# Three late attention units loaded in short runs and scored in 64 rows, a new order of the last output, and new lists for the first block

## The chip, the cores and the metric

The kernel runs on one core of a Trainium2 chip. The metric is device time in microseconds (us) of one execution; the kernel before takes 1649.12 us in the median of three runs (1648.95 to 1649.36).

Engines are named as the profile names them: PE is TensorE (matmul), PEld its weight loads, DVE is VectorE, ACT is ScalarE, POOL is GpSimd, SP is SyncE, which here only issues transfers. "SPq" and "ACTq" are the queues of transfers (DMAs) issued by SP and by ACT.

## The reference, cut to what matters

Three stages follow each other on 4608 tokens of width 512:

```python
# 1. attention in chunks of 64: q, k, v are (8 batches, 8 heads, 576, 64)
scores = scale * np.matmul(q_c, k_c.transpose(0, 1, 2, 4, 3))
attn = softmax(scores)                      # max subtracted, sum + 1e-9
out = np.matmul(attn, v_c)                  # -> x, (4608, 512)
# 2. gated layer, w_gate and w_val (512, 1536), w_out (1536, 512)
xn = x / sqrt(mean(x * x) + 1e-6) * rms_g
x = (silu(xn @ w_gate) * (xn @ w_val)) @ w_out
# 3. second layer, w_in (512, 2048), w_out (2048, 512)
h = x @ w_in
out = (h * clip(h + 3, 0, 6) / 6) @ w_out
```

## The kernel before

**Blocks.** The tokens go in nine blocks of 512. Every large matmul is done in split precision: an operand is a high and a low part of a narrower type, and three matmuls (high times high, low times high, high times low) make one product. From the third block on two blocks are multiplied together in a scheme that needs seven products where eight would be plain; the work of such a pair p is a row of `product` steps (the L1016 matmuls) and then 24 output steps (the triples L1030, L1031, L1033).

**The first block** runs from two lists written out by hand: `START` (attention of the first four 128-token tiles, mixed with the preparation of the first weights) and `FIRST` (the gated layer of block 0, mixed with more preparation). A token is one step: `scores1` is the scores of tile 1, `warm1` a matmul with no use for the result that keeps PE active, `Wm4`, `Wb4`, `Wh4`, `Wl4` the four steps that turn raw weight 4 into its high and low part (`Wb` is L201, L203 and L205 on DVE, `Wl` is L222 on DVE), `T` one tick of the general schedule (next paragraph). `LOADS` is the order of the first transfers. Each engine takes its instructions in the order of the list.

**The later attention** is cut into units of 256 tokens, numbered 4 to 17, and runs inside the ticks of the large products. Steps stand at fixed distances from a unit's first tick (`STEPS_P`): `turn_q` at 0, `turn_k` at 1 (a 32x32 transposition on DVE of the q and k that were loaded), scores at 3 and 5, values at 13. A unit is one of two classes:

- `Wide` loads q and k in runs of 2 KB with 8 DMAs (L886) of 128 KB each if the unit lies in one batch, with 16 smaller ones if a batch border cuts it. Its contraction over 64 is done in two accumulating matmuls of 32 rows, so the scores come in two groups of 64 matmuls (L910), at distance 3 and at distance 5, with a maximum (L921) after each.
- `Pair` loads q and k in runs of 128 bytes with 32 DMAs (L750) of 32 KB, and with 64 of 16 KB if a batch border cuts the unit in the middle, as it cuts 4 and 13. Its scores are one group of 32 matmuls of 64 rows (L781; the profile counts 64 records), all at distance 3, with one maximum (L791).

Units 4 to 9 are `Pair`; of the later ones those in `WHOLE`.

**Transfers.** q and k have one buffer each. The loads of unit i + 1 are handed to a supply when `turn_k` of unit i is issued, and each tick takes three DMAs from the supply (`some(3)`); whatever is left when `turn_q` of the unit comes is issued at once (`until`). The weights (`wo`, L463; `wd`, L469; 512 KB each) go on the same SP queue between them. SP takes its DMAs strictly in program order. The built program gives every DMA of SP and ACT one of eight completion semaphores in turn, and a DMA waits for the one that had its semaphore before, that is for the landing of the DMA eight places ahead of it.

**The end.** The last block's output accumulates in two halves of the features, m = 0 and m = 1. `last_out(m, cols, mid)` is 24 matmuls (L1796), and advances `mid` after the 15th. `tail` and `half_tail` scale a result into `c` on ACT (L1623, L1809), transpose it on PE (L1626, L1813), copy it and store it.

Of the kernel before, what the change touches and what calls it, by code (L numbers as in the profile page):

```python
# [18 lines left out]
def _f32_of(word):  # L19
# [7 lines left out]


LOADS = """
    q1 q3 q0 q2 w v3 w g w w v1 v0 v2 w w w w w w w w w w w w  # L30
""".split()
START = """
    warm2 warm2 warm2 warm2 warm2 warm2 warm2 warm2 warm2 warm2 trans_qk1 warm2 warm2 trans_qk3 out_k1 out_q1
    out_q3 out_k3 scores1 scores3 trans_qk0 warm2 trans_qk2 top1 top3 less3 less1 out_q0 expo3 out_k0 expo1 out_k2
    out_q2 total3 total1 share3 share1 scores0 warm1 warm1 warm1 warm1 scores2 trans_p3 top0 less0 top2 less2 Wm0
    out_p3 expo0 warm1 warm1 warm1 warm1 trans_p1 values3 out_p1 expo2 Wm1 out_x3 square3 total0 Wb0 total2 Wb1
    share0 share2 warm0 warm0 warm0 warm0 warm0 warm0 warm0 warm0 warm0 warm0 warm0 warm0 warm0 warm0 warm0 warm0
    warm0 warm0 warm0 warm0 mean3 trans_p0 warm2 warm2 warm2 warm2 warm2 warm2 warm2 warm2 values1 trans_p2 Wm2
    table3 out_p0 root3 Wm3 Wh0 out_p2 Wb2 inv3 values0 warm3 warm3 values2 spread3 out_x1 square1 square2 out_x2
    square0 mean1 mean2 root1 out_x0 root2 Wb3 norm3 inv1 inv2 warm3 warm3 warm3 spread1 mean0 spread2 root0 norm1  # L40
    inv0 warm3 warm3 warm3 warm3 warm3 spread0 norm2 norm0 Wm4 Wm6 hi3 hi1 hi2 hi0 Wh1 Wm5 Wh3 Wh2 lo3 Wl0 lo2 Wb6
    Wl1 Wl2 Wb4 Wl3 Wb5 lo1 lo0 warm1 warm1 warm1 warm1 warm1 warm1 warm1 warm1 warm1 warm1 warm1 warm1 warm1
    warm1 warm1 warm1 warm1 warm1 warm1 warm1
""".split()
FIRST = """
    G0 V0 T T S0 T M0 G1 T T Wm9 Wm8 Wm7 Wh4 T Wh5 A0 Wh6 Wb8 Wl4 Wb9 L0 Wl5 Wm10 Wm11 Wm13 S1 Wh9 V1 T M1 Wb10
    Wl6 Wb7 Wl9 A1 Wh7 Wh8 Wh10 L1 Wl7 D0 G2 Wb11 Wl8 V2 S2 D1 Wh11 Wm12 T M2 Wb13 Wm15 A2 Wl10 Wb12 G3 Wm19 Wm14
    Wh13 V3 Wl11 T L2 T Wh12 S3 Wl13 Wb14 Wl12 Wb15 Wb19 M3 D2 Wm18 T Wm16 Wh14 Wh15 G4 Wb18 A3 T Wm17 Wl14 L3
    Wb16 Wm22 S4 Wh18 Wm21 Wm25 V4 Wh16 T Wl15 Wb17 M4 Wb22 T Wl16 D3 T G5 Wh17 Wh22 A4 Wm24 L4 Wb25 Wb21 Wl17 V5
    T Wh19 S5 D4 Wm20 Wm26 Wh21 T Wm23 G6 Wl19 M5 Wb24 A5 Wl18 T Wb20 L5 Wl22 Wm31 Wh20 Wl20 V6 S6 T Wb26 Wl21 M6  # L50
    Wb23 A6 Wh23 Wh26 Wm27 Wh24 D5 T Wb31 L6 Wl26 Wb27 Wl23 T G7 V7 T S7 Wm28 D6 Wm33 T Wm29 Wm30 Wh25 G8 Wl24 M7
    Wb28 Wl25 A7 L7 Wb29 Wh27 T S8 V8 Wl27 M8 Wm32 Wh29 Wh28 A8 T Wb30 Wl29 Wl28 Wb33 T L8 Wm35 Wh33 Wm34 D7 G9
    Wb34 T V9 Wh30 T S9 D8 Wl33 Wl30 M9 Wh31 T T Wb32 G10 V10 T A9 Wh34 L9 Wl34 Wl31 Wh32 S10 M10 Wb35 Wl32 T A10
    D9 G11 T L10 S11 T V11 M11 D10 Wh35 A11 Wl35 L11 X T D11 T
""".split()
SHARE_V, LOW_V = (), (2, 3)

WHOLE = (10, 14)

STEPS_P = (  # L60
    (0, ("turn_q",)),
# [30 lines left out]
def fused_kernel(  # L92
# [20 lines left out]
    N = 512  # L113
# [983 lines left out]
    with tc.manual_schedule():  # L1097
# [8 lines left out]
        first = [Att(i) for i in range(NTL)]  # L1106
# [15 lines left out]

        unit = [(Pair if i < 10 or i in WHOLE else Wide)(i) for i in range(NPR)]
        chain = [Half(i) for i in range(NTL, 2 * NTL)] + unit[4:]
# [37 lines left out]
        def plan_unit(i, t0):  # L1162
            for d, steps in STEPS_H if i < NTL else STEPS if t0 < P0 else STEPS_P:
                for st in steps:
                    if i in WHOLE and st in ("scores0", "top0"):
                        st = st[:-1]
                    elif i in WHOLE and st in ("scores1", "top1"):
                        continue
# [44 lines left out]
        S00, S01, S11, S3, S1, S2, S4 = range(7)  # L1213
# [77 lines left out]
        A11, S2_, S1_, S3_, A12, S4_, A21, A22 = range(8)  # L1291
# [80 lines left out]
        for p in range(3):  # L1372
            b = 3 + 2 * p
            bk = {0: (2, 3), 1: (6, 7), 4: (4, 5)} if p % 2 == 0 else {0: (6, 7), 1: (2, 3), 4: (4, 5)}
            g = {}
# [11 lines left out]
            def bank(z, m):  # L1387
                return PS[:, bk[z][m], :]
# [3 lines left out]
            for i in range(NI + 1):  # L1392
# [5 lines left out]
                end = [(2, 0), (7, 0), (2, 1), (7, 1)]  # L1398
# [88 lines left out]
        X = {}  # L1487
# [133 lines left out]
        def tail(m, blk, h):  # L1621
            c, *o = [wp.tile([128, 2, N], F32, tag="w", name=n)[:, 0, :] for n in ("c", "ot", "ot")]
            nc.scalar.mul(c, bank(Z1, m), 1.0 / 6.0)  # L1623
            yield
            for n in range(NTL):
                nc.tensor.transpose(  # L1626
                    PS[:, ZT[n // 2], n % 2 * 128:(n % 2 + 1) * 128],
                    c[:, n * 128:(n + 1) * 128],
                    ident,
                )  # L1630
            f = h * 256 + m * 128
            for y, (e, q) in enumerate(((nc.scalar.copy, nc.scalar), (nc.vector.tensor_copy, nc.sync))):
                two = o[y][:, 0:256].rearrange("p (n f) -> p n f", n=2)
                e(two, PS[:, ZT[y], 0:256].rearrange("p (n f) -> p n f", n=2))
                r = blk * N + y * 256
                q.dma_start(out=out[r:r + 256, f:f + 128].rearrange("(n p) f -> p n f", p=128), in_=two)
# [30 lines left out]
        for b in range(1, NB, 2):  # L1667
# [5 lines left out]
            end = [(2, 0), (7, 0), (2, 1), (7, 1)]  # L1673
# [119 lines left out]
        def last_out(m, cols, mid):  # L1793
            for i in range(NQ):
                for wi, xi in ((0, 0), (1, 0), (0, 1)):
                    nc.tensor.matmul(  # L1796
                        bank(Z1, m)[:, cols],
                        stream.t[pb, "out", i // 2, O22][:, i % 2, wi, m * 128:(m + 1) * 128],
                        nx[i][xi][:, cols],
                        start=False,  # L1800
                        stop=False,
                        skip_group_check=True,
                    )
                if i == NQ // 2:
                    next(mid, None)

        def half_tail(y):
            c, o = [wp.tile([128, 2, N], F32, tag="w", name=n)[:, 0, 0:256] for n in ("c", "ot")]
            nc.scalar.mul(c, bank(Z1, 1)[:, y * 256:(y + 1) * 256], 1.0 / 6.0)  # L1809
            yield  # L1810
            z = PS[:, ZT[y], 256:512]
            for n in range(2):
                nc.tensor.transpose(z[:, n * 128:(n + 1) * 128], c[:, n * 128:(n + 1) * 128], ident)  # L1813
            e, q = ((nc.scalar.copy, nc.scalar), (nc.vector.tensor_copy, nc.sync))[y]
            two = o.rearrange("p (n f) -> p n f", n=2)
            e(two, z.rearrange("p (n f) -> p n f", n=2))
            r = b * N + y * 256
            q.dma_start(out=out[r:r + 256, 384:512].rearrange("(n p) f -> p n f", p=128), in_=two)

        last_out(0, slice(0, N), iter(()))  # L1820
        end = tail(0, b, 1)
        next(end)
        for y in range(2):
            last_out(1, slice(y * 256, (y + 1) * 256), end)
            end = half_tail(y)
            next(end)
        next(end, None)


# [28 lines left out]
```

## Time and profile before

| | us |
|---|---|
| median of three runs | 1649.12 |
| the profiled execution | 1649.82 |
| its span, first to last instruction | 1648.0 |
| PE busy in the span | 1636.9 |
| DVE, ACT, POOL busy | 1034.8, 846.0, 453.4 |
| granted TensorE clock, mean | 1.00 |

The 1.82 us between the profiled time and the span lie outside the instructions. Everything below is in us from the span's start. Roughly, `START` lasts to 33.5, `FIRST` to 155, the single blocks to 366, the first pair's products and outputs to 565, the other pairs to 915, and the second layer to the end.

### The profile page before, as it was taken

The numbers are of one execution on the slowest core, as the hardware profiler recorded it, in microseconds if no ns is written. First come the engines' busy times: TensorE is split into PE (matmuls) and PEld (weight loads), VectorE is DVE, ScalarE is ACT, GpSimd is POOL, SyncE is SP. The second block draws the span as 40 slices with busy tenths as digits, with TensorE's granted clock in tenths as the row PEclk, the third lists the DMA queues.
The fourth block names the chain that finished last, engine by engine and source line by source line (L and its number), as shares of the span: only waits on it lengthen the run. The fifth ranks groups of instructions, "written<-read, shape, count | busy, mean of one in ns | idle before, by whom it ended". The sixth has DMA issues, their size and how long they took to land.

```text
span 1648.0 us, 26265 instructions
## 1 busy us (share of the span) xinstructions
PE 1636.9 (99%) x9807; PEld 1348.0 (82%) x9807; DVE 1034.8 (63%) x1532; ACT 846.0 (51%) x1410; POOL 453.4 (28%) x331
## 2 busy tenths in 40 slices
PE   8999999999999999999999999999999999999998
PEld 7888887888888888788888888888888888888887
DVE  7997566655575755638334388358746764874475
ACT  6885445455454555645434344455545544654553
POOL 1002434322236423354226522140024003301310
PEclk9999999999999999999999999999999999999999
DMA  9914777748988698855979685667877796788666
GB/s 294 287 46 108 206 211 208 209 157 243 313 277 231 203 295 269 282 216 209 331 238 334 258 283 198 219 194 244 216 216 228 213 239 200 219 230 230 191 202 156
DMA packets 352223, 375.06 MB, mean 228 GB/s; under 512 B 201440, under 2 KB 277216, under 8 KB 351968
## 3 DMA queue, kind: packets, MB, share of 16 engines
q1 hardware_dynamic: 282208, 302.32, 60.2%
q10 hardware_dynamic: 69888, 71.06, 12.7%
q8 instruction: 78, 1.28, 0.3%
q14 instruction: 49, 0.40, 0.1%
HBM read 292.55 MB, written 80.74 MB: 227 GB/s over the span
## 4 chain that ended last, share of the span: by engine, by line
PE 93%; DVE 2%; DMA 2%; SPq 2%; issue 1%; ACT 1%; POOL 0%; ACTq 0%; DVEq 0%; POOLq 0%
PE PS L1016 37%; PE PS L1595 18%; PE PS L1005 13%; PE PS L1030 6%; PE PS L1031 6%; PE PS L1033 6%; SPq L750 1%; PE PS L1042 1%; PE PS L1039 1%; PE PS L1038 1%; PE PS L837 1%; DMA q<-in_q_dram 1%; PE PS L1796 1%; PE PS L819 1%; PE PS L910 1%
## 5 line engine op out<-in xcount | busy, mean ns | idle before, releaser
L1016 PE MATMUL PS<-xu,wo 128*128 128x512 f32 x1512 | 349.8, 391 | 0.7 <-DVE s L1370 0.7
L1016 PEld LDWEIGHTS PS<-xu,wo 128*128 128x128 f32 x1512 | 282.3, 188 | 60.3 <-DVE s L1370 1.1
L1016 PE MATMUL PS<-xo,wq 128*128 128x512 f32 x1344 | 305.3, 389 | 0.0
L1595 PE MATMUL PS<-gs,wq 128*128 128x512 f32 x1296 | 295.3, 389 | 0.0
L1016 PEld LDWEIGHTS PS<-xo,wq 128*128 128x128 f32 x1344 | 252.3, 188 | 52.4
L1595 PEld LDWEIGHTS PS<-gs,wq 128*128 128x128 f32 x1296 | 242.9, 188 | 51.8 <-DVE gs L1589 1.2
L1005 PE MATMUL PS<-XH,w 128*128 128x512 f32 x576 | 146.2, 395 | 1.0 <-DVE w L222 1.0
L1005 PEld LDWEIGHTS PS<-XH,w 128*128 128x128 f32 x576 | 106.2, 188 | 24.6 <-DVE w L222 1.8
L1030 PE MATMUL PS<-gs,wd 128*128 128x512 f32 x288 | 113.2, 393 | 0.0
L1031 PE MATMUL PS<-gs,wd 128*128 128x512 f32 x288 | 112.2, 390 | 0.0
L1061 POOL TENSOR_TENSOR al<-sg,ah 128x512 fp32r<-128x512 f32 x40 | 55.9, 1396 | 155.7 <-ACT ah L1059 149.9
L1366 POOL TENSOR_TENSOR gs<-gu,gs 128x512 fp32r<-128x512 f32 x60 | 84.5, 1427 | 46.2 <-ACT gs L1365 36.3
L1370 DVE TENSOR_TENSOR gu<-gu,PS 128x512 f32<-128x512 f32 x60 | 41.1, 686 | 84.4 <-ACT gu L1452 44.1
L1663 POOL TENSOR_TENSOR gt<-gx 128x512 f32<-128x512 f32 x8 | 10.4, 1294 | 296.5 <-DVE gx L1660 296.5
L1589 DVE TENSOR_TENSOR gs<-gu,gs 128x512 fp32r<-128x512 f32 x88 | 68.0, 792 | 31.9 <-ACT gs L1588 31.6
L1588 ACT CAST gs<-gt 128x512 fp32r<-128x512 f32 x96 | 58.2, 623 | 44.1 <-DVE gt L1732 30.7
L1525 DVE SCALAR_TENSOR_TENSOR gu<-gu,PS 128x512 f32<-128x512 f32 x48 | 32.8, 684 | 72.9 <-ACT gu L1522 72.9
L1005 PE MATMUL PS<-XL,w 128*128 128x512 f32 x288 | 77.2, 390 | 0.0
L1033 PE MATMUL PS<-gs,wd 128*128 128x512 f32 x288 | 77.0, 389 | 0.0
L1059 ACT CAST ah<-sg 128x512 fp32r<-128x512 f32 x52 | 32.4, 624 | 75.5 <-DVE sg L1350 41.3
L1588 ACT CAST gs<-gu 128x512 fp32r<-128x512 f32 x96 | 57.3, 620 | 25.0 <-DVE gs L1589 17.7
L1663 POOL TENSOR_TENSOR gt<-gu 128x512 f32<-128x512 f32 x24 | 32.6, 1359 | 129.0 <-DVE gu L1660 124.8
(254 smaller groups left out, 2828.0 us busy)
## 6 DMA issues: line engine op xcount, KB each, us to landing
wq<-stash_in SPq DMA_DIRECT2D x128, 512.0 KB
wo<-ops SPq DMA_DIRECT2D x126, 512.0 KB
wq<-sums_out SPq DMA_DIRECT2D x64, 512.0 KB
wq<-stash_out SPq DMA_DIRECT2D x48, 512.0 KB
wd<-keep_out SPq DMA_DIRECT2D x36, 512.0 KB
yd<-yst SPq DMA_DIRECT2D x18, 512.0 KB
ops<-w ACTq DMA_DIRECT2D x36, 256.0 KB
v<-in_v_dram SPq DMA_DIRECT2D x32, 256.0 KB
```

What stands on the lines that cost most here:

```text
L1005: nc.tensor.matmul(ps, w(wi, c), xs[c][xi], start=(i == 0), stop=(i == n - 1))
L1016: nc.tensor.matmul(PS[:, bank, :], op[:, wi, c * 128:(c + 1) * 128], x[xi][:, c, :], start=first and i == 0, stop=last and i == 5, skip_gr ...
L1030: nc.tensor.matmul(ps, wm[0], a[0], start=first, stop=False)
L1031: nc.tensor.matmul(ps, wm[1], a[0], start=False, stop=False)
L1033: nc.tensor.matmul(PS[:, banks[m], :], w[:, 0, m * 128:(m + 1) * 128], a[1], start=False, stop=last)
L1061: nc.gpsimd.tensor_tensor(lo, t, hi.bitcast(F32), op=ALU.subtract)
L1366: e.tensor_tensor(w[:, 1, :], t, w[:, 0, :].bitcast(F32), op=ALU.subtract)
L1370: nc.vector.tensor_tensor(o, x, y, op=op)
L1588: nc.scalar.copy(w[:, 0, :], x)
L1589: e.tensor_tensor(w[:, 1, :], x, w[:, 0, :].bitcast(F32), op=ALU.subtract)
L1595: nc.tensor.matmul(PS[:, banks[m], :], op[:, wi, m * 128:(m + 1) * 128], x[xi], start=first and (wi, xi) == (0, 0), stop=False, skip_group ...
L1663: nc.gpsimd.tensor_tensor(slot(i, "t"), slot(i, "12"), slot(i, "11"), op=ALU.subtract)
```

## The change

1. `WHOLE` grows from (10, 14) to (10, 12, 13, 14, 17): units 12, 13 and 17 become `Pair`.
2. The last output is done as half of m = 1, the whole of m = 0, the other half of m = 1; before it was the whole of m = 0 and then the two halves.
3. `LOADS`, `START` and `FIRST` are new orders of the same steps, with 77 warm matmuls where there were 79, and with six `Wb` tokens in `START` where there were seven. The rest of the program is the same.

```diff
 LOADS = """
-    q1 q3 q0 q2 w v3 w g w w v1 v0 v2 w w w w w w w w w w w w
+    q1 q3 q2 q0 w w g v3 w v1 w v0 v2 w w w w w w w w w w w w
 START = """
...
-    out_q3 out_k3 scores1 scores3 trans_qk0 warm2 trans_qk2 top1 top3 less3 less1 out_q0 expo3 out_k0 expo1 out_k2
+    out_q3 out_k3 scores1 scores3 trans_qk2 warm1 trans_qk0 top1 less1 top3 less3 expo1 out_q2 out_k2 expo3 out_q0
...
-    inv0 warm3 warm3 warm3 warm3 warm3 spread0 norm2 norm0 Wm4 Wm6 hi3 hi1 hi2 hi0 Wh1 Wm5 Wh3 Wh2 lo3 Wl0 lo2 Wb6
-    Wl1 Wl2 Wb4 Wl3 Wb5 lo1 lo0 warm1 warm1 warm1 warm1 warm1 warm1 warm1 warm1 warm1 warm1 warm1 warm1 warm1
+    warm3 warm3 warm3 warm3 warm3 warm3 spread2 norm0 norm2 Wh3 Wh0 hi1 Wh2 hi3 hi0 hi2 Wm5 Wm4 Wm8 Wl0 lo3 lo2
+    Wl1 Wl2 Wb5 Wl3 Wb8 lo1 lo0 warm1 warm1 warm1 warm1 warm1 warm1 warm1 warm1 warm1 warm1 warm1 warm1 warm1
...
 FIRST = """
-    G0 V0 T T S0 T M0 G1 T T Wm9 Wm8 Wm7 Wh4 T Wh5 A0 Wh6 Wb8 Wl4 Wb9 L0 Wl5 Wm10 Wm11 Wm13 S1 Wh9 V1 T M1 Wb10
+    G0 V0 T T S0 T M0 Wb4 G1 Wm9 Wh8 A0 Wh4 Wm7 Wm6 Wb9 Wl4 L0 Wb6 V1 T Wm13 Wh5 S1 T T Wm10 Wh6 Wl5 M1 Wb7 Wl6 D0
...
-WHOLE = (10, 14)
+WHOLE = (10, 12, 13, 14, 17)
...
-        last_out(0, slice(0, N), iter(()))
+        last_out(1, slice(0, 256), iter(()))
+        first = half_tail(0)
+        next(first)
+        last_out(0, slice(0, N), first)
         end = tail(0, b, 1)
         next(end)
-        for y in range(2):
-            last_out(1, slice(y * 256, (y + 1) * 256), end)
-            end = half_tail(y)
-            next(end)
+        last_out(1, slice(256, N), end)
+        end = half_tail(1)
+        next(end)
         next(end, None)
```

**Where instructions move: SP in the first pair.** These are SP's DMAs around the loads of unit 13 before the change; L886 loads q and k, `wo` and `wd` are weights.

```order
L886 DMA q<-in_q_dram 16x2x512 x3
L463 DMA wo<-ops_123 128x1024
L463 DMA wo<-ops_124 128x1024
L886 DMA q<-in_q_dram 16x2x512 x5
L886 DMA k<-in_k_dram 16x2x512
L463 DMA wo<-ops_124 128x1024 x2
L886 DMA k<-in_k_dram 16x2x512 x3
L463 DMA wo<-ops_124 128x1024
L886 DMA k<-in_k_dram 16x2x512 x4
L463 DMA wo<-ops_124 128x1024 x2
L469 DMA wd<-keep_out_125 128x1024
```

In the changed program the loads of unit 13 begin at the same place; after 24 of its q loads and the same seven `wo` SP goes on as follows, up to the v of the next unit.

```order
L469 DMA wd<-keep_out_125 128x1024
L469 DMA wd<-keep_out_126 128x1024
L750 DMA q<-in_q_dram 32x4x32 x6
L469 DMA wd<-keep_out_127 128x1024
L469 DMA wd<-keep_out_128 128x1024
L750 DMA q<-in_q_dram 32x4x32 x2
L750 DMA k<-in_k_dram 32x4x32 x4
L469 DMA wd<-keep_out_129 128x1024
L469 DMA wd<-keep_out_130 128x1024
L750 DMA k<-in_k_dram 32x4x32 x3
L469 DMA wd<-keep_out_131 128x1024
L750 DMA k<-in_k_dram 32x4x32 x25
```

The 16 loads were all ahead of the first `wd`; now 64 loads share the queue with seven `wo` and seven `wd`, and the last 25 of them stand in a row, put there by the `until` of unit 13's `turn_q`.

**PE at the end.** The last matmuls before the change:

```order
L1796 MATMUL PS<-gs,wq 128x512 x24
L1796 MATMUL PS<-gs,wq 128x256 x15
L1626 MATMUL PS<-ident,c 128x128 x4
L1796 MATMUL PS<-gs,wq 128x256 x24
L1813 MATMUL PS<-ident,c 128x128 x2
L1796 MATMUL PS<-gs,wq 128x256 x9
L1813 MATMUL PS<-ident,c 128x128 x2
```

and after it:

```order
L1796 MATMUL PS<-gs,wq 128x256 x24
L1796 MATMUL PS<-gs,wq 128x512 x15
L1813 MATMUL PS<-ident,c 128x128 x2
L1796 MATMUL PS<-gs,wq 128x512 x9
L1796 MATMUL PS<-gs,wq 128x256 x15
L1626 MATMUL PS<-ident,c 128x128 x4
L1796 MATMUL PS<-gs,wq 128x256 x9
L1813 MATMUL PS<-ident,c 128x128 x2
```

The matmuls are the same; the 512-wide ones now lie between the two 256-wide groups, and each scaled copy `c` is made while the next group runs.

**DVE at the start.** The first instructions of DVE, as a difference (`mx` is the maximum of a tile's scores, `v` the scores less it):

```order
 L1090 MEMSET one 128x1
 L1091 CAST ones_r<-one 128x256
-L546 TENSOR_REDUCE mx<-PS 128x8 x2
-L552 TENSOR_TENSOR v<-PS,mx 128x512 x2
+L546 TENSOR_REDUCE mx<-PS 128x8
+L552 TENSOR_TENSOR v<-PS,mx 128x512
+L546 TENSOR_REDUCE mx<-PS 128x8
+L552 TENSOR_TENSOR v<-PS,mx 128x512
 L560 TENSOR_REDUCE sm<-v 128x8
```

The two maxima no longer follow each other, and the first one now waits for a later place of PE's stream: in the changed list `warm1`, which writes the bank of tile 1, stands behind the eight transposes of `trans_qk2` and ahead of `top1`.

## Rows read from the trace of the kernel before

**Rows 1.** The page: PE's busy time, and its costliest wait.

```profile
PE 1636.9 (99%) x9807; PEld 1348.0 (82%) x9807; DVE 1034.8 (63%) x1532; ACT 846.0 (51%) x1410; POOL 453.4 (28%) x331
L1005 PE MATMUL PS<-XH,w 128*128 128x512 f32 x576 | 146.2, 395 | 1.0 <-DVE w L222 1.0
```

**Rows 2.** Timeline of PE around groups of scores: start, duration, instruction, count.

```profile
377.29 1.16 PE L781 MATMUL PS<-kT,qT 64*64 64x64 f32 x64
462.68 1.16 PE L910 MATMUL PS<-kT,qT 32*64 32x64 f32 x64
463.77 5.75 PE L1016 MATMUL PS<-xu,wo 128*128 128x512 f32 x24
469.45 1.16 PE L910 MATMUL PS<-kT,qT 32*64 32x64 f32 x64
505.63 1.16 PE L910 MATMUL PS<-kT,qT 32*64 32x64 f32 x64
```

**Rows 3.** Chain that ended last, a stretch of products that nothing interrupts.

```profile
366.46 10.89 PE PS L1016 x48
```

**Rows 4.** Timeline of PE and of DVE at the end: [idle before, releaser].

```profile
1631.11 7.39 PE L1796 MATMUL PS<-gs,wq 128*128 128x512 f32 x39
1631.42 1.89 DVE L1589 TENSOR_TENSOR gs<-gt,gs 128x512 fp32r<-128x512 f32 x3
...
1640.48 2.05 PE L1796 MATMUL PS<-gs,wq 128*128 128x256 f32 x15 [0.47 <-ACT c L1809]
```

**Rows 5.** Timelines of DVE and PE in the first 40 us.

```profile
1.25 2.50 PE L640 MATMUL PS<-ones_r 128*128 128x256 f32 x10 [1.25 <-DVE ones_r L1091]
...
8.27 1.43 DVE L546 TENSOR_REDUCE mx<-PS 128x8 f32<-128x512 f32 x2 [7.08 <-PE PS L535]
...
9.65 0.36 PE L640 MATMUL PS<-ones_r 128*128 128x256 f32 x1
...
16.16 2.66 PE L640 MATMUL PS<-ones_r 128*128 128x256 f32 x20
...
35.45 1.20 PE L1005 MATMUL PS<-XH,w 128*128 128x512 f32 x4 [0.77 <-DVE w L222]
...
35.92 0.42 DVE L201 TENSOR_SCALAR wtmp<-wtmp 128x512 f32<-128x512 f32 x1
36.37 0.43 DVE L203 TENSOR_SCALAR wtmp<-wtmp 128x512 uint32<-128x512 uint32 x1
36.83 0.69 DVE L205 SCALAR_TENSOR_TENSOR wraw<-wraw,wtmp 128x512 uint32<-128x512 uint32 x1
```

**Rows 6.** Windows inside `FIRST`: length, busy time (instructions) by engine, clock, DMA share, GB/s.

```profile
60.00:80.00 20.00, 20.00 (x152) 16.17 (x151) 19.13 (x39) 15.62 (x39) 0.00 (x0) 1.00 0.94 307
```

**Rows 7.** Timeline of SP: issue of the first, until the last, DMA, count.

```profile
123.06 16.32 SPq L750 DMA_DIRECT2D k<-in_k_dram  x32
...
415.71 1.28 SPq L886 DMA_DIRECT2D q<-in_q_dram  x3
...
460.51 1.28 SPq L886 DMA_DIRECT2D q<-in_q_dram  x3
...
479.00 0.84 SPq L463 DMA_DIRECT2D wo<-ops  x2
...
501.94 1.42 SPq L750 DMA_DIRECT2D q<-in_q_dram  x3
...
514.59 9.35 SPq L750 DMA_DIRECT2D k<-in_k_dram  x14
```

**Rows 8.** Waits of SP's queue from 455 to 530: us in total, times, longest.

```profile
SPq L469 <- DMA wo<-ops: 3.8, 2, 2.0
```

**Rows 9.** Chain from 150 to 180, a transfer of 256 KB from issue to landing.

```profile
174.38 2.22 DMA ops<-oh
```

**Rows 10.** Transpositions on DVE: timeline before unit 13's loads, and group of the short form.

```profile
458.22 2.27 DVE L890 STREAM_TRANSPOSE qT<-q 128x1024 f32<-128x1024 f32 x1
L762 DVE STREAM_TRANSPOSE kT<-k 128x1024 f32<-128x1024 f32 x8 | 9.7, 1209 | 0.0
```

More of the change, by code (lines that the diff above doesn't have):

```diff
@@ L29 @@
 LOADS = """
-    q1 q3 q0 q2 w v3 w g w w v1 v0 v2 w w w w w w w w w w w w
+    q1 q3 q2 q0 w w g v3 w v1 w v0 v2 w w w w w w w w w w w w
 """.split()
 START = """
-    warm2 warm2 warm2 warm2 warm2 warm2 warm2 warm2 warm2 warm2 trans_qk1 warm2 warm2 trans_qk3 out_k1 out_q1
-    out_q3 out_k3 scores1 scores3 trans_qk0 warm2 trans_qk2 top1 top3 less3 less1 out_q0 expo3 out_k0 expo1 out_k2
-    out_q2 total3 total1 share3 share1 scores0 warm1 warm1 warm1 warm1 scores2 trans_p3 top0 less0 top2 less2 Wm0
@@ L36 @@
[L36 to L40, printed above, removed]
@@ L41 @@
-    inv0 warm3 warm3 warm3 warm3 warm3 spread0 norm2 norm0 Wm4 Wm6 hi3 hi1 hi2 hi0 Wh1 Wm5 Wh3 Wh2 lo3 Wl0 lo2 Wb6
-    Wl1 Wl2 Wb4 Wl3 Wb5 lo1 lo0 warm1 warm1 warm1 warm1 warm1 warm1 warm1 warm1 warm1 warm1 warm1 warm1 warm1
+    warm0 warm0 warm0 warm0 warm0 warm0 warm0 warm0 warm0 warm0 trans_qk1 warm0 warm0 trans_qk3 out_k1 out_q1
+    out_q3 out_k3 scores1 scores3 trans_qk2 warm1 trans_qk0 top1 less1 top3 less3 expo1 out_q2 out_k2 expo3 out_q0
+    out_k0 total1 total3 share1 share3 scores2 warm3 warm3 scores0 trans_p1 warm3 warm3 warm3 warm3 trans_p3 top2
@@ new lines @@
+    less2 top0 less0 out_p1 expo2 Wm0 out_p3 expo0 warm2 warm2 warm2 warm2 warm2 warm2 warm2 warm2 warm2 warm2
+    warm2 values3 warm0 warm0 warm0 warm0 warm0 warm0 warm0 warm0 warm0 warm0 warm0 warm0 warm0 warm0 warm0 warm0
+    values1 Wm1 out_x3 table3 square3 Wm2 square1 out_x1 total2 Wb0 total0 Wb1 share2 share0 trans_p2 mean3
+    trans_p0 mean1 root3 out_p2 out_p0 root1 Wm3 Wb2 inv3 inv1 warm2 values0 spread3 values2 square0 out_x0
+    square2 out_x2 warm1 mean0 spread1 mean2 root0 Wh1 root2 Wb3 norm3 inv0 norm1 inv2 spread0 warm3 warm3 warm3
@@ L45 @@
 FIRST = """
-    G0 V0 T T S0 T M0 G1 T T Wm9 Wm8 Wm7 Wh4 T Wh5 A0 Wh6 Wb8 Wl4 Wb9 L0 Wl5 Wm10 Wm11 Wm13 S1 Wh9 V1 T M1 Wb10
[L47 to L54, printed above, removed]
+    G0 V0 T T S0 T M0 Wb4 G1 Wm9 Wh8 A0 Wh4 Wm7 Wm6 Wb9 Wl4 L0 Wb6 V1 T Wm13 Wh5 S1 T T Wm10 Wh6 Wl5 M1 Wb7 Wl6 D0
+    A1 Wh7 Wh9 Wm14 T Wm11 Wl7 L1 Wl8 Wb10 G2 Wb13 V2 D1 T T S2 Wb14 Wl9 M2 Wm15 T Wh10 Wm18 Wm12 A2 G3 Wb15 Wl10
+    L2 Wb11 Wb12 T Wh13 Wm16 Wh11 V3 D2 S3 Wm19 Wb18 Wl11 Wb16 Wl13 M3 Wh18 Wh14 T Wh12 Wl12 Wh16 Wh15 Wm21 A3
+    Wl15 Wl18 L3 G4 Wm22 S4 T Wm17 V4 Wl14 Wl16 Wb19 Wb21 M4 Wb17 A4 Wm20 Wh17 Wh21 D3 T T Wl17 L4 Wb22 Wb20 G5 V5
+    Wm26 T S5 Wm23 D4 Wb23 M5 Wh19 T A5 Wm29 Wh20 Wh22 G6 Wb26 Wb29 T Wm27 Wl22 Wl19 L5 Wh29 Wh23 S6 V6 T Wl20
+    Wl21 M6 Wb27 Wm28 Wm24 Wh26 Wm32 A6 T Wl23 Wb24 L6 Wl26 D5 G7 T V7 Wm25 T D6 Wh24 S7 Wh27 T G8 Wl24 Wb25 M7
+    Wl29 Wh25 Wb28 Wl25 Wb32 Wm33 Wm31 A7 T Wb31 L7 Wm30 S8 V8 T Wb33 Wb30 M8 Wl27 A8 Wh28 Wm35 Wh30 D7 L8 T Wl28
+    T G9 V9 T S9 Wh31 Wm34 D8 T G10 Wb35 M9 Wb34 A9 Wl30 T L9 T Wl31 Wh33 V10 S10 Wh32 M10 Wl33 Wl32 Wh34 A10 Wh35
+    T D9 G11 Wl34 L10 Wl35 S11 V11 T D10 T M11 T A11 L11 X D11 T
 """.split()
 SHARE_V, LOW_V = (), (2, 3)
-WHOLE = (10, 14)
+WHOLE = (10, 12, 13, 14, 17)
 STEPS_P = (
```

## The prediction

> **What bounds the kernel now.** I read the page first: PE is busy 1636.9 of 1648.0 us, and of its few waits the largest kind after the start is 1.0 us in all, for prepared weights [rows 1]. So only three things can move the time: matmuls that PE no longer does, waits at the two ends of the program where PE isn't yet or no longer covered, and a new wait that is put into the covered middle. Then I read the timeline of PE around the groups of scores [rows 2, 3], the two ends [rows 4, 5], and last the queue of SP, because the three changed units load q and k in four times as many DMAs as before, 32, 64 and 32 instead of 8, 16 and 8 [rows 7, 8]. The reader is to see there that SP's is the only queue whose work this change multiplies.
>
> **Scores: −4.0 us.** A `Wide` unit's second group starts 1.09 us before the products go on (462.68 to 463.77 [rows 2]). It also interrupts them: the 24 products between the two groups take 5.68 us (463.77 to 469.45 [rows 2]) where 24 uninterrupted ones take 10.89 / 2 = 5.45 [rows 3], so another 0.23. A `Pair` unit's single group of 64 records takes 1.16 us like one of the two [rows 2]. So a unit saves 1.09 + 0.23 = 1.32 us, three of them 4.0, all on PE, which never waits there. DVE's part (transposition 1.21 instead of 2.2 us [rows 10]) gets shorter too, and hides.
>
> **Last output: −0.5 us.** Before, PE stood 0.47 us between the two halves until ACT had scaled the first [rows 4]. Now 15 matmuls of 512 columns lie over that copy, and the copy of m = 0 lies under 15 of 256 columns, which took 2.05 us [rows 4]. The last half with its copy, transposes and store is as before. What could eat this: the half pass goes through its operands twice as fast, and the last of them come out of DVE at 1633.31 (1631.42 + 1.89 [rows 4]). The last output starts at 1631.11, and at the pace of 15 matmuls in 2.05 us [rows 4] the half pass is at its 17th of 24 by then, about where it needs them. I keep bounds of −0.7 and +0.3.
>
> **Start lists: +1.0 us.** DVE sets the pace up to the first real matmul. Before, its first maximum starts at 8.27; in the changed list it waits for a warm matmul behind eight transposes, and that place of PE's stream was over at 9.65 + 0.36 = 10.01 [rows 5]. That is 1.7 later. One `Wb` less in `START` takes 0.42 + 0.43 + 0.69, less the overlaps 1.4 us, off DVE [rows 5]; so the first matmuls come 0.3 later. That step is now done in `FIRST`, where DVE is busy 19.13 of 20 us [rows 6]: of its 1.4 us half may come through to PE, 0.7. The wait of 0.77 for prepared weights [rows 5] is for the same kind of step as before, and I leave it in. Bounds: −1.0 if both waits of [rows 1] go and `FIRST` hides all, +2.5 if it hides nothing.
>
> **Loads of units 12 and 17: 0.** Each has 32 DMAs of 32 KB instead of 8. Unit 12's begin at 415.71 [rows 7] with some 12 weight loads between; at the 0.65 us derived below, 44 DMAs are through by 444.3, and `turn_q` stood at 458.22 [rows 10]. Unit 17 has the same distance one pair later. If they had no such room, each microsecond late would be one of PE.
>
> **Loads of unit 13: +7.9 us.** The q buffer comes free when unit 12 has been transposed: 458.22 + 1.2 [rows 10], so the first of the 64 is issued at about 459.5. PE wants the scores at 505.63 [rows 2], 1.32 sooner by unit 12's saving: 504.3 (the shift of the start moves both). Between stand 64 loads and 14 weight loads, 78 DMAs, in program order. What does one cost? Nothing else to carry: 32 in 16.32 us, 0.51 each, of the same size [rows 7]. Beside weights, in the next unit: from 501.94 to 523.94 (514.59 + 9.35) SP issued 16 q, 14 k and four `wd`, 34 in 22.0 us, 0.65; its k alone 14 in 9.35, 0.67 [rows 7]. In the very stretch, 460.51 to 479.84, it issued 16 q and k of 64 KB and seven `wo`, 23 in 19.3 us, 0.84 [rows 7]. The surplus over 0.51 is the wait for the DMA eight places ahead: SP waited there for the landing of `wo`, up to 2.0 us at a time [rows 8]. So I take 0.65 for the 53 DMAs up to the last `wd` of this stretch, 34.4 us, to 493.9; and 0.59, midway between 0.51 and 0.67, for the 25 k in a row, which only ACT's transfers disturb, 14.8 us, to 508.7. Landing takes 2.2 us more (a 256 KB transfer did, [rows 9]; I have no row for a small one), `turn_k` 1.2 [rows 10] and 0.1 of handing over: the scores can start at 512.2, and PE stands 7.9 us. It takes its instructions in order, and behind the scores it has only the outputs of this pair, so nothing fills the hole. By the cheapest row (0.51 throughout) the scores are ready at 499.3 + 3.5 = 502.8 and the wait is nothing; by the dearest (0.84 for the 53, then 0.67) at 524.3, and it is 20.
>
> **Sum.** −4.0 − 0.5 + 1.0 + 7.9 = +4.4. On the profiled execution (1649.82, 0.70 above the median shown) 1654.2; on the median 1649.12 it is 1653.5, +0.27%. A measurement of this kernel tells about 0.2%, 3.3 us, from no change.
>
> **Rivals.**
> - *SP keeps its unloaded pace, and nothing stalls.* It decides at (504.3 − 3.5 − 459.5) / 78 = 0.53 us per DMA: at or under that, PE never waits, and the time is 1649.12 − 3.5 = 1645.6, faster. For it: unit 4's loads, of this very shape, went at 0.51 [rows 7]. Against it: they had no weight loads between them, and every stretch with weights shows 0.65 or more. Chance 0.28, and it falls on both sides of the bound of 0.2% (1645.8) by what the start lists do.
> - *A small stall,* 1 to 5 us, from a pace of 0.54 to 0.59: 1646.6 to 1650.6, no change that can be told. Chance 0.17.
> - *The pause also costs clock.* In the first microseconds, after PE had been idle, ten warm matmuls took 2.50 us, 0.21 apart from the first on, where later 20 took 2.66, 0.12 apart [rows 5]; these are the two levels, 1.2 and 2.4 GHz (the granted-clock column says 1.00 in every slice and doesn't show it). The slow ones reach past 3.3 us, and the single one at 9.65 is too late to tell. If the stall puts PE back to 1.2 GHz for as long as that start shows at least (1.25 to 3.75), half of that stretch, 1.3 us, is lost, and about 2.5 if it lasts twice as long: 1654.8 to 1656. No pause in the trace after the start is longer than 1 us, so no row tells whether it happens. The Trainium skill, page "TensorE: Matmul & The Clock Gate", section "HAM oscillation — how this bites in real kernels", says that a PE which waits for DMA between stretches of matmuls falls back to the lower clock and starts the next stretch at it; by that rule the sum would be these 1.3 to 2.5 us higher. Chance 0.25, together with a stall of the size forecast.
> - *A long stall,* 11 to 20 us, by the dearest row, with weights for the next steps late behind it: 1657 to 1666. Chance 0.08.
> - *The forecast itself,* a stall of 5 to 11 us and no more: 1650.6 to 1656.6, chance 0.22 alone and 0.47 with the one that also loses clock, which shares its place and its mechanism.
>
> **How the numbers follow.** The likeliest is the stall of about 8 us: 1653.5. The range has to reach to the case without a stall, 1645.6 less half a microsecond for the lists, 1645, and up to a stall of 12 with lost clock, 1661; that leaves some 2 in 10 out. The likeliest case's own range is 1650 to 1658. Faster by over 0.2%: the part of the first rival with hidden lists, 0.22. Within 0.2%: the rest of it, the small stalls and the low end of the forecast, 0.28. Slower: 0.50.
>
> **What would show it.** In the profile after: half as many L910 groups as before, six instead of twelve, three more of L781, and products without a break where the second groups were; no wait of PE for `c` between the halves; SP's row of 25 k of unit 13 ending near 508, a `turn_k` (L762) just behind the last landing, and a wait of PE at L781 near 504 with kT of L762 as releaser, followed by matmuls at twice their spacing if the clock fell. The first L1005 near 34 and the end of `FIRST` about 1 us later. I am wrong if SP issues those 78 DMAs at 0.53 us each or faster, if PE waits at units 12 or 17 instead, or if the lists move the first block by more than 2.5 us.

## The result, and the profile after

The changed kernel takes 1662.41 us in the median of five runs (1660.34 to 1666.58), the kernel before beside it 1649.36 (1648.95 to 1652.23): a ratio of 1.0078, 95% interval 1.0066 to 1.0090. It is 13 us slower, where 4.4 us slower were forecast. The profiled execution took 1663.08 us, its span 1661.3.

The page's first line and PE's costliest waits of the changed kernel (in a list of waits: us in all, times, longest):

```profile
PE 1637.8 (99%) x9613; PEld 1349.1 (81%) x9613; DVE 1025.1 (62%) x1529; ACT 847.0 (51%) x1410; POOL 455.4 (27%) x331
```

```profile
PE PS L781 <- DVE kT L762: 11.8, 1, 11.8
PE PS L519 <- DMA q<-in_k_dram: 2.5, 2, 2.2
PE PS L1005 <- POOL XL L647: 1.6, 1, 1.6
PE PS L640 <- DVE ones_r L1091: 1.2, 1, 1.2
PE PS L1016 <- DMA wo<-ops: 1.0, 1, 1.0
```

PE has 194 instructions fewer than in [rows 1] (three second groups of 64 and two warm matmuls), and one new wait of 11.8 us, longer than all of its waits in the trace of before together. It is the one at unit 13's scores. Timelines of SP, DVE and PE there:

```profile
463.46 1.33 SPq L750 DMA_DIRECT2D q<-in_q_dram  x3
...
496.36 1.77 SPq L469 DMA_DIRECT2D wd<-keep_out  x2
498.50 1.36 SPq L750 DMA_DIRECT2D k<-in_k_dram  x3
499.95 0.65 SPq L469 DMA_DIRECT2D wd<-keep_out  x1
500.65 14.76 SPq L750 DMA_DIRECT2D k<-in_k_dram  x25
```

```profile
502.95 1.23 DVE L762 STREAM_TRANSPOSE qT<-q 128x1024 f32<-128x1024 f32 x1
519.03 1.25 DVE L762 STREAM_TRANSPOSE kT<-k 128x1024 f32<-128x1024 f32 x1 [14.86 <-DMA v<-in_v_dram]
```

```profile
507.50 1.07 PE L1033 MATMUL PS<-gs,wd 128*128 128x512 f32 x4
520.33 1.99 PE L781 MATMUL PS<-kT,qT 64*64 64x64 f32 x64 [11.76 <-DVE kT L762]
522.25 0.79 PE L1030 MATMUL PS<-gs,wd 128*128 128x512 f32 x1
522.84 0.63 PE L1031 MATMUL PS<-gs,wd 128*128 128x512 f32 x1
523.26 0.63 PE L1030 MATMUL PS<-gs,wd 128*128 128x512 f32 x1
...
525.18 1.07 PE L1033 MATMUL PS<-gs,wd 128*128 128x512 f32 x4
```

One chain explains it: q is there in time (its transposition at 502.95), the issue of the last of the 25 k in a row ends at 515.41, k is transposed 3.6 us later, and PE goes on at 520.33. (The profile infers what ended a wait from semaphores, and loads of k and v use the same ones; the transposition reads k and not v.) Then the scores take 1.99 us instead of 1.16 [rows 2], and the next matmuls start 0.43 apart, where the same ones were 0.23 apart before (507.06, 507.29, 507.52 in that trace): PE is on the lower clock. The windows of that stretch say so too (length, busy time and instructions of PE, PEld, DVE, ACT, POOL, granted clock, DMA share, GB/s):

```profile
500.00:510.00 10.00, 8.57 (x38) 6.76 (x36) 3.25 (x3) 1.92 (x3) 3.04 (x3) 1.00 0.60 177
510.00:515.00 5.00, 0.00 (x0) 0.00 (x0) 0.00 (x0) 0.00 (x0) 0.00 (x0) 0.58 0.22 34
515.00:520.00 5.00, 0.00 (x0) 0.00 (x0) 0.97 (x1) 1.69 (x3) 2.49 (x2) 0.50 0.92 243
520.00:525.00 5.00, 4.67 (x72) 4.04 (x73) 3.63 (x6) 1.38 (x3) 1.26 (x1) 0.56 1.01 298
525.00:530.00 5.00, 5.00 (x24) 4.14 (x23) 0.34 (x1) 0.94 (x2) 3.80 (x3) 1.00 0.96 265
```

From 510 to 520 not one matmul runs, the granted clock falls to the lower level (0.50), and the DMA engines are at 0.22 of their time in the first half: what PE waits for is small transfers being issued one by one, not bandwidth. The chain that ended last shows SP at it in the burst, and the list of SP's waits from the first load of unit 13 to the last what else it did:

```profile
511.19 0.43 SPq L750
511.66 0.43 SPq L750
```

```profile
SPq L750 <- DMA wd<-keep_out: 5.3, 4, 2.7
SPq L750 <- DMA wo<-ops: 3.4, 4, 1.1
```

From 504.97 on SP starts a load every 0.47 us without a wait, 0.43 of it issuing. Over the whole stretch (463.46 to 515.41, 52.0 us) its waits for landings add up to 14.3 us and those for PE to 1.0, which leaves 0.47 for each of the 78 transfers.

I set the same PE instructions of the two traces beside each other and read how much later each starts: 2.4 us at the first L1005, 3.9 at the first product (366), 2.9 behind unit 12's scores, 14.7 at unit 13's scores and 16.5 from the sixth matmul behind them on, 15.2 where its second group stood, 13.9 behind unit 17's, 13.3 at the last transposes. So the wait and its clock are 13.6, the three second groups give 1.0, 1.3 and 1.3, the last output 0.66, and the start is 3.9 later.

### The profile page after: what moved, and what is told of

Same layout as the page of the kernel before. It is cut to its first block, busy times and chain, and to the rows that moved or that the text cites. A ratio compares the mean times of both kernels' runs of the same rounds, so it can differ in the third digit from the quotient of the medians.

```text
span 1661.3 us, 25966 instructions
## 1 busy us (share of the span) xinstructions
PE 1637.8 (99%) x9613; PEld 1349.1 (81%) x9613; DVE 1025.1 (62%) x1529; ACT 847.0 (51%) x1410; POOL 455.4 (27%) x331
## 4 chain that ended last, share of the span: by engine, by line
PE 89%; DMA 5%; SPq 2%; DVE 2%; ACT 1%; issue 1%; POOL 1%; ACTq 0%; DVEq 0%; POOLq 0%
PE PS L1016 37%; PE PS L1595 18%; PE PS L1005 12%; PE PS L1030 5%; PE PS L1031 5%; PE PS L1033 5%; SPq L750 2%; DMA q<-in_q_dram 1%; PE PS L1042 1%; PE PS L1038 1%; PE PS L1039 1%; DMA k<-in_k_dram 1%; PE PS L837 1%; PE PS L1796 1%; DMA wo<-ops 1%
## 5 line engine op out<-in xcount | busy, mean ns | idle before, releaser
L1005 PE MATMUL PS<-XH,w 128*128 128x512 f32 x576 | 146.2, 395 | 0.1
L1005 PEld LDWEIGHTS PS<-XH,w 128*128 128x128 f32 x576 | 106.2, 188 | 23.5 <-ACT XH L994 1.3
L1030 PE MATMUL PS<-gs,wd 128*128 128x512 f32 x288 | 113.7, 395 | 0.0
L1005 PE MATMUL PS<-XL,w 128*128 128x512 f32 x288 | 77.4, 390 | 1.6 <-POOL XL L647 1.6
```

What stands on the lines that cost most here:

```text
L1005: nc.tensor.matmul(ps, w(wi, c), xs[c][xi], start=(i == 0), stop=(i == n - 1))
L1030: nc.tensor.matmul(ps, wm[0], a[0], start=first, stop=False)
```

## The experiments

**Each part alone.** Four runs, measured beside the kernel before (median 1649.45 us). The edits:

```diff
whole_only: -WHOLE = (10, 14)
            +WHOLE = (10, 12, 13, 14, 17)
tail_only:  only the new order of last_out
lists_only: only LOADS, START and FIRST
no13 (against the changed kernel, the others against the kernel before):
            -WHOLE = (10, 12, 13, 14, 17)
            +WHOLE = (10, 12, 14, 17)
```

> The kernel before with WHOLE of the change alone (units 12, 13, 17 become Pair). Theory: the wait at unit 13's scores comes of its 64 loads among 14 weight loads on SP, whatever the start does: wait of about 11.8 us at L781, matmuls behind it at the lower clock for some 4 us (2 us lost), less 1.2 us for each of three second groups of scores; in sum +10, about 1659.5. Rival, that the wait needs the later start of the changed lists: no wait, 3.6 us gained, about 1645.7.

Measured: 1663.51 us, ratio 1.0087 (1.0073 to 1.0101). The units alone make the whole loss, with the old start, and 4 us more than the 1659.5 expected. In its trace PE's waits lead with

```profile
PE PS L781 <- DVE kT L762: 14.9, 1, 14.9
```

longer than in the changed kernel: here SP took 54.7 us from the first q (461.86) to the last k (516.55), where it took 52.0 in the profiled execution above; 15.8 us of it were waits for landings, where those were 14.3. The size of the wait differs by 3 us between the two traces; with one trace of each kernel it isn't shown whether the program or the execution makes that difference. The rival falls.

> The kernel before with the new order of the last output alone. Theory: the wait of 0.47 us for c between the halves goes and the operands are ready in time: 0.5 to 0.7 us faster, about 1648.7. Rival, that the half pass waits for the last operands from DVE or that the last stores queue: no gain, 1649.4.

Measured: 1648.63 us, ratio 0.9999 (0.9990 to 1.0008): by the time alone the gain can't be told. The trace shows it, though: the last output starts 1.10 us earlier than in the trace of before and the last transposes 1.76 earlier, so 0.66 is gained between, and in the changed kernel 13.92 and 13.26 give 0.66 again. The list of PE's waits no longer has L1796 in it. The rival falls by the trace.

> The kernel before with the new LOADS, START and FIRST alone. Theory: the lists cost what the two traces differ by at the start of the first pair, 3.9 us: 1653.2, with the first L1005 some 2.4 us later, a wait for POOL's XL behind it, and part of it regained in FIRST. Rival, that the late landing of the third tile's q and k in the one profiled execution was chance: about 1650.5 in the median, as the recorded sum had it.

Measured: 1650.83 us, ratio 1.0008 (0.9996 to 1.0019): 1.4 us, near the rival's figure, and not clear of zero. The theory's 1653.2 falls. In this run's trace the first product starts 2.0 us later than in the trace of before, not 3.9, and there is no wait for XL: a good part of the 3.9 was chance; more on it below.

> The changed kernel with unit 13 taken out of WHOLE again. Theory: units 12 and 17 are loaded in time, so the wait and the lower clock go (13.6 us) and the 1.2 us for unit 13's second group come back: about 1650.0, PE without a wait at any L781. Rival, that four times the loads are too many at 12 or 17 too: a wait at their scores, over 1652.

Measured: 1648.83 us, ratio 0.9997 (0.9988 to 1.0006). With unit 13 left as it was, the time is 13.6 us under the changed kernel's, so the whole loss of 13 is gone; no PE wait at an L781 is left in its trace. The theory stands: 12 and 17 are loaded in time.

**Unit 13 alone, its count, and the count without unit 13.** The edits, each against the kernel before:

```diff
only13:  +WHOLE = (10, 13, 14)
half13:  +WHOLE = (10, 13, 14), and in Pair.parts_qk
-                                for a in range(NP):
+                                for a in range(NP // 2 if self.i == 13 and src is k else NP):
...
+            if self.i == 13 and dst is self.k:
+                nc.sync.dma_start(out=dst[:, 512:1024], in_=...)
split12: +WHOLE = (10, 12, 14), and in Pair.parts_qk
+                            elif self.i == 12:
+                                for a in range(NP):
+                                    for z in range(0, un, 4):
+                                        nc.sync.dma_start(
+                                            out=d[r:r + 32, a, u0 + z:u0 + z + 4, :], in_=sv[j, g, :, a, z:z + 4]
+                                        )
+                                        yield
```

> The kernel before with unit 13 alone made Pair. Theory: the 64 loads of unit 13 are the whole of the loss: wait at its L781 some 1.3 us shorter than the 14.9 of the run with units 12, 13 and 17, since PE comes 1.3 us later, the same 2 us at the lower clock, one second group of scores saved: +14 to +15, about 1664. Rival, that units 12 and 17 carry part of it (their loads push unit 13's or the weights behind): under 1660.

Measured: 1661.88 us beside 1651.77 for the kernel before on that chip, ratio 1.0065 (1.0047 to 1.0083); PE waits 11.6 us at L781. Ten us, where 14 to 15 were expected: the interval ends at 13.7, so the theory's figure is missed, and the time alone doesn't refute the rival (its bound lay 10.5 above the kernel before). Against the 14 of the run with all three the intervals overlap. The trace decides more: beside that of before, PE's instructions are 1.7 us later ahead of unit 13's scores, 15.5 behind them and the lower clock, and no further loss follows. Unit 13 alone makes a loss of that size; whether 12 and 17 add up to 2 us to its wait stays open.

> As the run before, but half of unit 13's k (16 of its 32 loads) comes in one load of 256 KB from another place, so the outputs of that unit are not the reference's. Theory, that the number of SP's transfers sets the end at 0.57 to 0.70 us each: 15 fewer take 8.6 to 10 us off, a wait of 4 to 6 us stays, about 1653 to 1655. Rival, that the end is set by the weights' transfers between them or by the DMA engines' bytes, which stay as they are: the wait shrinks by 3 us at most, over 1659.

Measured: ratio 1.0028 (1.0016 to 1.0040), 1656.9 us beside 1651.77, 5.1 above it. The scores of unit 13 in its timeline, and PE's windows around them:

```profile
512.65 1.16 PE L787 MATMUL PS<-kT,qT 64*64 64x64 f32 x64 [3.58 <-DVE kT L768]
```

```profile
512.00:514.00 2.00, 1.35 (x65) 1.28 (x66) 1.45 (x4) 0.62 (x1) 0.00 (x0) 1.00 1.11 341
514.00:518.00 4.00, 4.00 (x12) 3.08 (x12) 2.96 (x3) 1.72 (x3) 2.66 (x3) 0.57 1.08 323
```

Fifteen loads fewer take 8.0 us off the wait (11.6 to 3.6), 0.54 each. The scores run at their usual 1.16, but the clock falls right behind them (0.57 from 514 to 518), and PE is 1.6 us later behind that stretch than at the scores. The weights between are the same, the bytes are the same, the count is not: the rival falls. One thing besides the count changed, since the load of 256 KB also has runs of 2 KB instead of 128 bytes; the next run keeps the runs.

> The kernel before with unit 12 made Pair and its 32 loads of 32 KB cut into 64 of 16 KB, the same runs of 128 bytes and the same bytes. Theory: a wait appears at unit 12's L781 though no batch border cuts it: 64 loads and 12 weights from 415.7 at 0.70 us end at 469, landing and transposing 5 more, PE is there at 462.7: a wait of about 11 us and 2 us of lower clock, about 1661. Rival, that it was the border, the place in the program or the 128-byte runs and not the count: no wait, 1648.1.

Measured: ratio 1.0084 (1.0065 to 1.0103), 1664.02 us beside 1651.77. Its timelines of SP and PE:

```profile
416.87 1.29 SPq L751 DMA_DIRECT2D q<-in_q_dram  x3
...
461.57 12.40 SPq L751 DMA_DIRECT2D k<-in_k_dram  x25
```

```profile
477.13 1.99 PE L788 MATMUL PS<-kT,qT 64*64 64x64 f32 x64 [13.21 <-DVE kT L769]
```

This is the strongest of the runs: unit 12 lies in one batch and is harmless with 32 loads; with the same bytes in the same runs of 128, cut into 64 loads, it makes a wait, a lower clock (scores in 1.99 instead of 1.16) and a loss like unit 13's. From 416.87 to 473.97 SP issued 64 loads and 14 weights, 0.73 each. The rival falls.

**More loads per tick.** The burst of 25 looks as if the three per tick were at fault.

```diff
supply6: +WHOLE = (10, 13, 14)
-            some(8 if t < 0 else 5 if t < P0 - 14 else 3)
+            some(8 if t < 0 else 5 if t < P0 - 14 else 6)
```

> The kernel before with unit 13 alone made Pair, and six loads of q and k taken in each tick of this stage where it was three, so that none of the 64 is left for the burst at the end. Theory, that SP's queue is full and the order of its 78 transfers hardly matters: the last k is issued at 508 to 512 as before, PE stands 7 to 12 us in all, part of it now for wd instead of at L781; about 1658 to 1662. Rival, that three per tick leave 25 for a burst and this alone makes the wait: no wait over 1 us, about 1650.

Measured: 1667.14 us, ratio 1.0102 (1.0089 to 1.0116): slower than with the burst (1.0047 to 1.0083 for unit 13 alone), and beyond the 1662 expected. The issue of the last k ends at 504.94, not at 508 to 512 as expected: the order does move the loads. The wait at L781 is nearly gone, and PE waits elsewhere instead. Its list of PE's waits, that of ACT's from 470 to 520, and PE's windows behind the longest of the waits:

```profile
PE PS L1030 <- ACT gs L1365: 3.8, 3, 1.6
PE PS L1016 <- ACT s L1457: 3.4, 1, 3.4
PE PS L1016 <- DVE ge L1370: 2.1, 1, 2.1
...
PE PS L781 <- DVE kT L762: 0.9, 1, 0.9
```

```profile
ACT gu L1361 <- DMA k<-in_k_dram: 8.4, 1, 8.4
ACT gs L1365 <- DMA stash_in<-shi: 6.0, 1, 6.0
...
ACT gs L1365 <- DMA k<-in_k_dram: 4.7, 1, 4.7
```

```profile
493.00:497.00 4.00, 2.79 (x7) 2.21 (x8) 0.69 (x1) 2.58 (x4) 1.98 (x2) 0.54 0.94 315
497.00:500.00 3.00, 3.00 (x19) 1.96 (x21) 0.00 (x0) 0.00 (x0) 0.55 (x1) 0.50 0.25 46
```

The rival falls, and the theory gets a second half that its expectations had left out: ACT issues transfers too, they take their turn at the same eight semaphores, and so ACT stands until loads of k have landed, with the arithmetic behind it in its stream. With the burst ACT stands for k as well (13.2 us at L1365 in the changed kernel), but there PE is standing anyway. In both ways of dealing out the 64 loads PE lost by them, directly or through ACT; a third way wasn't tried, and the six per tick hold for the later units too. The trace, beside that of before, splits the loss of this execution, 14.9 us from the first product on: 3.4 are the wait for ACT at L1457, about 3 the lower clock behind it, 3.8 three waits for ACT at L1030, 0.9 the wait at L781, 2.1 a wait for DVE at 616, less 1.3 for the second group; the rest lies in smaller pieces. The median is 3 us above the profiled execution, which no trace splits.

**What is left when unit 13 is left out.** The first run, and three beside each other:

```diff
best, best_again: the kernel before with WHOLE = (10, 12, 14, 17) and the new last_out
no13_again:       the same with the new LOADS, START and FIRST
best16:           best with WHOLE = (10, 12, 14, 16, 17)
```

> The kernel before with units 12 and 17 made Pair and the new order of the last output, old lists and unit 13 as before. Theory: two second groups (2.5) and the wait at the end (0.6) are gained and nothing lost: 1646.3, no PE wait at an L781. Rival, that the loads of 12 or 17 delay weights: a wait of PE for wo of 1 us or more eats half of it, 1648.

Measured: 0.9986 (0.9976 to 0.9996), 1648.97 us beside 1651.77.

> Units 12 and 17 and the last output, old lists, once more, to stand beside the same with the new lists. Theory: 0.1 to 0.2% faster than before, as in its first run.

Measured: 0.9990 (0.9981 to 0.9998), 1648.14 us beside 1649.86. Faster both times, by 1.7 to 2.8 us, a little less than the 3.1 expected. No PE wait at an L781 and none for `wo` is listed in the first run's trace, and two for `wo` of 1.2 us in all in the second's, which may be part of that.

> The same with the new lists, so that the pair of runs gives the cost of the lists. Theory, by the run of the lists alone (1.4 us) and the recorded sum (1.0): 1 to 2 us above the one with the old lists. Rival, by the difference of the two first traces (3.9 us at the start of the first pair): 3 to 4 us above it.

Measured: 1.0001 (0.9992 to 1.0010), 1649.84 us, 1.7 us above the version with the old lists. With the 1.4 us of the lists alone, two comparisons put the lists between 1 and 2 us; neither interval by itself excludes zero, and 3 us lie at the upper edge of both. The rival is unlikely, not excluded.

> Units 12, 16 and 17 made Pair, the new last output, the old lists. Theory: unit 16 has 32 loads and the room of 14 ticks like 12 and 17, so another 1.3 us: 1.3 us below the version with 12 and 17, no wait at an L781. Rival: three units in a row keep SP's queue so full that wo comes late, PE waits 1 to 3 us for wo in the second pair, and nothing is left of the gain.

Measured: 0.9975 (0.9965 to 0.9986), 1646.04 us beside 1649.86: 3.8 us faster than the kernel before and 2.1 faster than the version without unit 16, where 1.3 were expected; the intervals of those two versions overlap, so unit 16's share isn't clear of noise. No wait for `wo` stands among PE's: the rival finds no support. In its timeline of SP the loads of units 16 and 17 are through in time:

```profile
618.60 1.97 SPq L750 DMA_DIRECT2D q<-in_q_dram  x3
...
648.70 1.30 SPq L750 DMA_DIRECT2D k<-in_k_dram  x2
...
662.00 1.32 SPq L750 DMA_DIRECT2D q<-in_q_dram  x3
...
694.30 0.92 SPq L750 DMA_DIRECT2D k<-in_k_dram  x2
```

This version beats both kernels. It has the change's gains at units 12 and 17 and at the last output, one unit more, and neither the cut unit nor the lists.

## Why the prediction was wrong

The direction and the mechanism were right, the size was not: 1653.5 was forecast, and 1662.4 lies outside the range, which ended at 1661. The step that failed is the sum's term for the loads of unit 13, +7.9, with the clock behind it left out of the sum: together they measured 13.6 in the trace of the changed kernel and 16.7 in that of the units alone. The outcome is the rival of a long stall (11 to 20 us, 1657 to 1666), which had a chance of 0.08. Step by step:

- **Scores, −4.0.** Three times 1.32 were forecast; the trace gives 1.0, 1.3 and 1.3. Right. Units 12 and 17 cost no wait, as the step on their loads had it, though by less room than it had: unit 12's loads and the weights between took 0.81 us each (43 from 419.57 to 454.21), not 0.65, and `turn_q` followed at 462.08.
- **Last output, −0.5.** 0.66 in both traces. Right; the operands from DVE were ready.
- **Start lists, +1.0.** 1.4 and 1.7 us in the two comparisons. Right within what can be measured, but not by the steps given. The first L1005 was forecast near 34 and starts between 34.2 and 35.9 in four traces with the new lists. The wait for prepared weights, which I left in, went; in three of the four a wait of 1.6 us for POOL's XL, which I had not seen, took its place:

```profile
39.61 0.73 PE L1005 MATMUL PS<-XL,w 128*128 128x512 f32 x2 [1.64 <-POOL XL L647]
```

- **Loads of unit 13, +7.9.** This step failed, by its size. It was the right wait at the right place, and two terms were short. The 53 transfers ahead took 37.2 us (463.46 to 500.65) instead of 34.4, 0.70 each: I had the pace from the next unit, where a `wd` stands between three loads, and here they come in twos (that this makes the difference isn't shown). Landing and handing over took 3.6 us instead of 2.3: I had no row for a small transfer and took one of 256 KB; in the other runs with 64 loads it took from 1.8 (split12) to 3.9 (whole_only). Both together, less the 0.3 us that PE came later than forecast, make the 11.8 of the trace. The 25 k in a row took 14.76 us where 14.8 was worked out, and that was partly luck: 0.59 each was a middle value, while SP issued them at 0.47 with one wait of 2.7 for a `wd`, and other runs show 12.4 to 15.3. In the trace of the units alone, with 54.7 us for the 78 transfers, the wait is 14.9.
- **What sets the pace.** The prediction put the surplus over 0.51 down to SP waiting for the landing of `wo`, by [rows 8]. Those two waits stand at L469 and so behind the stretch meant, whose weights are `wo`. Of SP's waits inside that stretch in the trace of before, the longest is for a transfer that ACT issues (`stash_in`):

```profile
SPq L463 <- DMA stash_in<-slo: 4.7, 1, 4.7
SPq L886 <- DMA wo<-ops: 2.3, 2, 1.7
```

  The cause was of the right kind, a landing ahead, but transfers of ACT count too.
- **The clock** fell, as the rival with chance 0.25 had it (there with a stall of the size forecast): the sum should have carried it. Its cost was 1.8 us (14.7 us later at the scores, 16.5 from the sixth matmul behind them on), within the 1.3 to 2.5 worked out from the first matmuls of the program. So the rule of the Trainium skill, page "TensorE: Matmul & The Clock Gate", section "HAM oscillation — how this bites in real kernels", which I had left to a rival, agrees with this trace: granted clock 0.50 at the end of the pause and 0.56 in the 5 us behind it, and the first matmuls about twice as far apart. In half13, with a pause of 3.6 us, the scores still ran at full clock and the fall came behind them.
- **Sum.** With 13.6 to 16.7 instead of 7.9 for unit 13 and its clock, 3.6 for the scores and 1.5 for the lists: −3.6 − 0.7 + 1.5 + 13.6 = +10.8, and up to +13.9. The measured 13.05 lies in that.

The rival that SP keeps its unloaded pace of 0.51 is refuted by every run of 64 loads in threes: 0.66 to 0.73 per transfer where weights stand between. SP's own issue, 0.47, would have kept under the 0.53 at which nothing stalls; the waits for landings brought it over. What stays open is why these waits differ from trace to trace (14.3 us in the changed kernel, 15.8 with the units alone), and the lists' cost to better than 1 us.

## What to carry to other kernels

When an edit multiplies small transfers, count what stands in program order between the moment their buffer is free and the moment they are needed, weights included, and hold the count times the loaded pace of that very stretch against the room; here bytes and DMA share (0.22 while PE stood) didn't show it. In this program a transfer that waits for one eight places ahead makes its whole engine wait, so dealing the same transfers out more evenly moved the wait to an engine that computes. If the forecast has PE standing, carry the lower clock behind the pause in the sum: behind PE's waits of 3.4 to 14.9 us it cost some 1.6 to 3 us here. And check each unit of a group by itself: two of three gained, and the third took back about five times their gain.

## What was not expected

The start of the program differs from trace to trace by more than the lists change it. Nine kernels here share every list and load up to the first pair's products (the kernel before and eight of the runs), and the first product starts between 366.30 (the kernel before, the earliest) and 370.57 (best16):

```profile
366.30 11.05 PE L1016 MATMUL PS<-xu,wo 128*128 128x512 f32 x48
```

```profile
370.57 11.04 PE L1016 MATMUL PS<-xu,wo 128*128 128x512 f32 x48
```

Four kernels with the new lists lie between 367.84 and 370.24. One part of it are the waits of PE for the first k, here in three kernels with the old lists: the units 12, 13 and 17, unit 13 alone, and the first run of the version without it:

```profile
PE PS L519 <- DMA q<-in_k_dram: 1.9, 1, 1.9
```

```profile
PE PS L519 <- DMA q<-in_k_dram: 2.6, 2, 1.8
```

```profile
PE PS L519 <- DMA q<-in_k_dram: 2.1, 1, 2.1
```

The kernel before had 0.7 us of it in its trace, the changed one 2.5. Behind such a pause the clock can be lower: in the changed kernel it is 0.55 and 0.60 from 12 to 20, in the run of 13 alone, with 2.6 us of waits, it stays at 1.00.

```profile
12.00:16.00 4.00, 2.99 (x42) 2.32 (x46) 3.79 (x10) 2.75 (x6) 1.55 (x2) 0.55 0.94 249
16.00:20.00 4.00, 4.00 (x50) 3.88 (x51) 2.82 (x5) 1.94 (x4) 0.54 (x1) 0.60 1.05 287
```

So a comparison of two traces at the start, which gave 3.9 us for the lists, needs the medians beside it, which gave 1.4 and 1.7.
